# Seven half products in place of eight in the down-projection of a fused RetNet and SwiGLU kernel

## The chip, the cores and the metric

The kernel runs on one core of a Trainium2 chip. A core has TensorE (PE, matrix products, with a queue of weight loads shown as PEld), VectorE (DVE), ScalarE (ACT), GpSimd (POOL) and SyncE (SP, which issues transfers and DMA transposes). PE writes its results into PSUM, eight banks of 128 partitions by 2 KB; DVE and ACT read PSUM, POOL does not. Each engine takes its instructions strictly in the order of its own list, and waits on semaphores for the others.

The metric is the device time of one execution in microseconds (us), lower is better, as a median of several runs. The profile is of one execution, on its own clock: its span goes from the first to the last instruction.

## The reference, cut to what matters

```python
batch, n_heads, seq, head_dim = (4, 8, 768, 64)          # attention
n_tokens, d_model, d_ff = (3072, 512, 1536)              # feed-forward

def _attn_ref(q, k, v):
    gamma = 1.0 - 2.0 ** (-5.0 - np.arange(H))
    for t in range(S):
        state = gamma * state + einsum('bhd,bhe->bhde', k[:, :, t], v[:, :, t])
        y[:, :, t] = scale * einsum('bhd,bhde->bhe', q[:, :, t], state)
    return y

def _moe_ref(x, w_gate, w_val, w_out, rms_g):
    xn = x / sqrt(mean(x * x, axis=-1) + 1e-06) * rms_g
    g = xn @ w_gate
    silu = g * (1.0 / (1.0 + np.exp(-g)))
    val = xn @ w_val
    return (silu * val @ w_out)
```

`x` is the attention's output, one row of 512 values for each of the 3072 tokens. The last product, `(silu * val) @ w_out`, is the down-projection: rows of 1536 values by a 1536 x 512 matrix.

## The kernel before, in words

The sequence is cut into 6 chunks of 128 positions. Chunk c of all four batches together is **group** c: 512 tokens. For a group the attention is done in chunk form: products of queries and keys (`a`), a mask on DVE (`m0`, `m1`; tile `am`), their product with the values together with the state's share (`z`, `w`; tile `y_ps`), and the update of the state (`k`; tile `kv_ps`, with the decayed values `vp` made by `V`). Then come the mean square on ACT (`S`), its inverse root on POOL (`R`; tiles `ms`, `rstd`), the normalised rows on DVE (`N`; tile `xn`), and their transpose by DMA (`XE`; tile `xnT`).

The feed-forward part of a group is cut along d_ff into 12 slices n of 128. For each slice there is a gate product `g` and a value product `v`, each four matmuls with 512 moving columns (the tokens) and the weights as the loaded operand; `s` takes the SiLU on ACT, and `h` multiplies both on DVE into `hT`, which is [128, 12 slices, 512 tokens] in bf16.

The down-projection `d` of a batch b of the group takes, for each of the 12 slices, 128 tokens of `hT` as loaded operand and the slice's 512 columns of `wo_b` (w_out in bf16) as moving operand, and adds all 12 in one PSUM bank: 12 matmuls of 512 columns, 48 for a group. `o` copies the bank to SBUF on ACT or DVE, `st` stores it. Batch 3 of the last group is cut by columns into 192, 192 and 128 (`e`), so that the last copy and store are small.

What sets the order of the work is one text, `ORDER`, written out by hand or by a planner: a list of steps such as `d.1.2.0.12/1`, which is step `d` with c=1, b=2, slices 0 to 12, in PSUM bank 1, or `V.3.0@D`, step `V` on DVE. The program is recorded in this order, and each engine gets its share of it in this order; nothing is moved later. A step may wait for a tile that is not ready, and everything behind it on its engine waits with it.

The lines that the prediction speaks of: matmuls of `g` and `v` L665, of `d` L695, of `e` L721; `am` L471, `w` L522, `k` L485; `vp` L383, `xn` L595, `ms` and `rstd` L581 and L583; copies L142.

Of the kernel before, what the change touches and what calls it, by code (L numbers as in the profile page):

```python
# [54 lines left out]
v.2.6.7.0.4/4 g.2.7.8.0.4/5 g.2.5.6.0.4/3 g.2.4.5.0.4/6 v.2.1.2.0.4/0 R.3.0 R.3.1 h.2.6.7.0.4 N.3.1 Cq.3.2@P
h.2.1.2.0.4 N.3.0 V.3.2@P s.2.8.9.0.4 s.2.7.8.0.4 s.2.5.6.0.4 g.2.0.1.0.4/5 v.2.7.8.0.4/1 v.2.8.9.0.4/2 v.2.5.6.0.4/3
g.2.2.3.0.4/0 k.3.1/47 tq.3.3 tk.3.3 tk.3.2 Lv.4.2@S tq.3.2 Lv.5.2@S Lq.5.3@S XE.3.1@S Lq.4.0@S Cq.5.3@P V.4.2@D
h.2.5.6.0.4 h.2.7.8.0.4 u0.3.1 h.2.8.9.0.4 s.2.4.5.0.4 s.2.2.3.0.4 b0.3.1@A s.2.0.1.0.4 v.2.0.1.0.4/3 v.2.4.5.0.4/1
v.2.2.3.0.4/2 z.3.1/50 a.3.1/46 u1.3.1 h.2.4.5.0.4 m0.3.1 m1.3.1 h.2.0.1.0.4 Cq.5.2@D h.2.2.3.0.4 g.2.10.11.0.4/1
v.2.9.10.0.4/4 w.3.1 g.2.9.10.0.4/3 v.2.11.12.0.4/6 v.2.10.11.0.4/2 g.2.11.12.0.4/7 S.3.2 s.2.9.10.0.4 S.3.3  # L60
s.2.10.11.0.4 s.2.11.12.0.4 Lk.4.3@P R.3.2 R.3.3 N.3.2 h.2.9.10.0.4 N.3.3 h.2.10.11.0.4 h.2.11.12.0.4 Lv.5.3@S
XE.3.0@S tq.4.1 Lv.4.0@S st.0.0@S XE.3.2@S Lv.4.1@S XE.3.3@S st.0.1@S Lv.4.3@S Lq.4.2@S d.2.1.0.10/4 d.2.1.10.12
d.2.2.0.12/6 d.2.3.0.12/2 g.3.11.12.0.4/7 v.3.0.1.0.4/0 g.3.0.1.0.4/1 g.3.6.7.0.4/5 g.3.10.11.0.4/3 st.0.3@S Lq.4.3@S
tk.4.0 st.1.0@S o.2.3@A s.3.6.7.0.4 o.2.2@A s.3.0.1.0.4 V.5.3@D o.2.1@A V.4.3@D h.3.0.1.0.4 V.4.1@P s.3.11.12.0.4
s.3.10.11.0.4 g.3.3.4.0.4/5 g.3.2.3.0.4/6 v.3.11.12.0.4/4 v.3.10.11.0.4/3 v.3.6.7.0.4/7 g.3.4.5.0.4/0 v.3.3.4.0.4/1
g.3.1.2.0.4/2 Cq.4.3@D h.3.10.11.0.4 h.3.11.12.0.4 V.4.0@D h.3.6.7.0.4 s.3.3.4.0.4 s.3.4.5.0.4 s.3.1.2.0.4 Cq.4.2@P
# [30 lines left out]
def kernel(  # L97
# [11 lines left out]
    nc = tc.nc  # L109
# [88 lines left out]
    def ring(shape, dtype, name, bufs):  # L198
        return sb.tile(shape, dtype, name=name, bufs=bufs)
# [506 lines left out]
    def st(e, bk, c, b, i=None):  # L706
# [4 lines left out]
        else:  # L711
            e.dma_start(out=out_h[c, b // 2, b % 2][:, :, m], in_=x)


    CUT = (0, 192, 384, 512)

    @op
    def e(e, bk, c, b, i):
# [42 lines left out]
```

## Time and profile before

| | us |
|---|---|
| median of 3 runs | 228.56 (228.42 to 229.04) |
| span of the profiled execution | 227.3 |
| PE busy | 221.2 (97%) |
| DVE busy | 121.5 (53%) |
| ACT busy | 88.0 (39%) |
| POOL busy | 88.2 (39%) |
| mean granted clock of PE | 1.000 |

The profiled execution's own time is known by its span alone: 227.3 us, 1.26 us below the median of the runs shown. Busy times are sums over an engine's instructions; a matmul's listed duration (380 ns for 512 columns) holds its way through a pipeline, so the pace of matmuls is read from the chain, where a row gives the time that so many took one behind the other.

### The profile page before, as it was taken

What the parts mean: (1) busy time and instruction counts of PE and PEld (TensorE: products, weight loads), DVE (VectorE), ACT (ScalarE), POOL (GpSimd) and SP (SyncE); (2) the same over time, 40 slices, a digit from 0 to 9 for tenths busy, and PEclk for the clock granted to TensorE, in tenths of its full rate; (3) what the DMA queues carried; (4) which work ended last, traced back from release to release, by engine and by line L of the source; (5) the groups of instructions that cost most, each with busy time, mean ns of one, the idle gap of its engine ahead of it and who ended that gap; (6) DMA issues with size and microseconds to landing.
All of it is one profiled execution on the core that took longest, in us unless ns stands there. A gap on an engine that the chain in (4) does not pass through costs nothing.

```text
span 227.3 us, 5786 instructions
## 1 busy us (share of the span) xinstructions
PE 221.2 (97%) x2410; PEld 115.0 (51%) x2410; DVE 121.5 (53%) x224; ACT 88.0 (39%) x192; POOL 88.2 (39%) x137
## 2 busy tenths in 40 slices
PE   7899999999999999999999999999999999999994
PEld 2577854565455644444444445544554444444453
DVE  6495459946388685247751377850564543052211
ACT  7798323341525540724411545251452232152011
POOL 8899897746632640743225803170031000000000
PEclk9999999999999999999999999999999999999999
DMA  6999999999999986999969999556003400220116
GB/s 130 174 164 180 197 172 193 177 187 200 186 145 159 182 119 146 248 143 219 154 163 257 163 159 218 130 102 136 2 6 87 144 0 4 91 92 0 46 52 227
DMA packets 105355, 31.57 MB, mean 139 GB/s; under 512 B 94449, under 2 KB 102385, under 8 KB 105330
## 3 DMA queue, kind: packets, MB, share of 16 engines
q0 software_dynamic: 40112, 9.70, 46.4%
q1 hardware_dynamic: 65218, 21.51, 44.1%
q8 instruction: 19, 0.31, 0.6%
q14 instruction: 6, 0.05, 0.1%
HBM read 28.31 MB, written 6.29 MB: 152 GB/s over the span
## 4 chain that ended last, share of the span: by engine, by line
PE 87%; DMA 4%; DVE 2%; issue 2%; POOL 2%; SPq 0%; ACT 0%; POOLq 0%
PE g_ps L665 26%; PE v_ps L665 26%; PE o_ps L695 25%; DMA qb<-in_q_dram 2%; DMA qf<-in_q_dram 2%; PE o_ps L721 1%; DVE am L535 1%; PE kv_ps L485 1%; PE a_ps L428 1%; PE y_ps L522 1%; PE y_ps L506 1%; PE y_ps L550 1%; PE t_ps L396 1%; PE t_ps L391 1%; PE xt_ps L608 1%
## 5 line engine op out<-in xcount | busy, mean ns | idle before, releaser
L665 PE MATMUL v_ps<-xnT,wv_b 128*128 128x512 bf16 (+2 forms) x344 | 70.0, 345 | 0.0
L665 PE MATMUL g_ps<-xnT,wg_b 128*128 128x512 bf16 (+2 forms) x344 | 69.7, 345 | 0.0
L676 ACT ACTIVATE sg<-g_ps 128x512 bf16<-128x512 f32 (+2 forms) x76 | 41.9, 577 | 67.0 <-PE g_ps L665 54.4
L695 PE MATMUL o_ps<-wo_b,hT 128*128 128x512 bf16 x276 | 62.6, 380 | 0.0
L686 DVE TENSOR_TENSOR hT<-sg,v_ps 128x512 bf16<-128x512 bf16 x48 | 32.8, 723 | 38.7 <-ACT sg L676 19.4
L665 PEld LDWEIGHTS <-wv_b 128*128 128x128 bf16 x344 | 30.8, 98 | 30.2 <-DVE hT L686 0.4
L665 PEld LDWEIGHTS <-wg_b 128*128 128x128 bf16 x344 | 30.3, 98 | 29.3 <-DVE st_f L494 0.2
L695 PEld LDWEIGHTS <-hT 128*128 128x128 bf16 x276 | 26.2, 98 | 29.8
L595 DVE SCALAR_TENSOR_TENSOR xn<-y_ps,rstd,g_bc 128x512 bf16<-128x512 f32 x24 | 17.6, 746 | 12.7 <-POOL rstd L583 12.1
L688 DVE TENSOR_TENSOR hT<-sg,v_ps 128x512 bf16<-128x512 bf16 (+2 forms) x28 | 16.6, 606 | 14.6 <-PE v_ps L665 7.5
L364 POOL TENSOR_TENSOR qb<-qf,ydec 128x512 bf16<-128x512 f32 x13 | 13.7, 1065 | 26.9 <-DMA qf<-in_q_dram 26.9
L142 ACT COPY o_sb<-o_ps 128x512 f32<-128x512 f32 (+2 forms) x17 | 9.2, 553 | 36.6 <-PE o_ps L695 32.3
L567 ACT ACTIVATE xsq<-y_ps 128x512 f32<-128x512 f32 x24 | 14.2, 596 | 21.6 <-PE y_ps L506 16.2
L336 POOL DMA_DIRECT2D kb<-in_k_dram x20 | 18.2, 911 | 2.6 <-DMA wo_b<-in_moe_w_out_dram 1.4
L581 POOL TENSOR_SCALAR ms<-ssq 128x1 f32<-128x1 f32 x21 | 4.4, 212 | 35.1 <-ACT xsq L567 30.0
L471 DVE TENSOR_TENSOR am<-a_ps,causal_h 128x512 bf16<-128x512 f32 x16 | 10.6, 684 | 8.9 <-PE a_ps L462 8.9
L142 DVE COPY o_sb<-o_ps 128x512 f32<-128x512 f32 (+1 forms) x9 | 5.7, 647 | 13.8 <-PE v_ps L665 4.8
L583 POOL TENSOR_TENSOR rstd<-ms,mhalf 128x1 f32<-128x1 f32 x21 | 11.6, 551 | 1.7
L535 DVE TENSOR_TENSOR am<-a_ps,mask 128x512 bf16<-128x512 f32 x16 | 10.2, 681 | 2.4 <-PE a_ps L428 2.3
L383 POOL TENSOR_TENSOR vp<-vf,vdec 128x512 bf16<-128x512 f32 x7 | 7.3, 1050 | 7.9 <-DMA vf<-in_v_dram 7.9
L383 DVE TENSOR_TENSOR vp<-vf,vdec 128x512 bf16<-128x512 f32 x9 | 6.2, 692 | 4.5 <-DMA vf<-in_v_dram 4.5
L229 PE MATMUL hot_ps<-one 128*128 128x512 bf16 x16 | 6.2, 523 | 1.0 <-DVE one L149 1.0
(99 smaller groups left out, 166.4 us busy)
## 6 DMA issues: line engine op xcount, KB each, us to landing
out_dram<-o_sb SPq DMA_DIRECT2D x23, 256.0 KB, 2.4
vf<-in_v_dram SPq DMA_DIRECT2D x17, 256.0 KB, 3.6
qf<-in_q_dram SPq DMA_DIRECT2D x16, 256.0 KB, 4.1
kb<-in_k_dram POOLq DMA_DIRECT2D x23, 128.0 KB, 6.1
wo_b<-in_moe_w_out_dram POOLq DMA_DIRECT2D x3, 512.0 KB, 10.7
qb<-in_q_dram POOLq DMA_DIRECT2D x8, 128.0 KB, 7.4
vp<-in_v_dram POOLq DMA_DIRECT2D x7, 128.0 KB, 10.1
wv_b<-in_moe_w_val_dram POOLq DMA_DIRECT2D x3, 256.0 KB, 6.2
```

What stands on the lines that cost most here:

```text
L142: return (e.copy if e is ACT else e.tensor_copy)(out, in_)
L336: i = done[n, c, b] = e.dma_start(out=x, in_=rows[n][b, c])
L364: e.tensor_tensor(out=u["qb"], in0=u["qf"], in1=ydec[:, c, :, None].to_broadcast([128, H, D]), op=ALU.mult)
L383: e.tensor_tensor(out=u["vp"], in0=u["vf"], in1=vdec[:, c, :, None].to_broadcast([128, H, D]), op=ALU.mult)
L535: return DVE.tensor_tensor(out=u["am"][:, i], in0=u["a"][i], in1=m, op=ALU.mult)
L567: return ACT.activation(xsq, flat(u["y"]), AF.Square, accum_out=u["ssq"])
L595: return DVE.scalar_tensor_tensor(out=u["xn"], in0=flat(u["y"]), scalar=u["rstd"], in1=g_bc, op0=ALU.mult, op1=ALU.mult)
L665: r = nc.tensor.matmul(p[:, (n - n0) * m:(n - n0 + 1) * m], W[w][0][:, s, n * 128:(n + 1) * 128], xnT[c][:, s, b0 * C:b1 * C], start=s == ...
L676: return ACT.activation(sg[:, :cols], done["wg", c, n0, b0][:, :cols], AF.Silu)
L686: return DVE.tensor_tensor(out=out, in0=sg, in1=p, op=ALU.mult)
L688: return DVE.tensor_tensor(out=hT[c][:, n0:n1, b0 * C:b1 * C], in0=sg, in1=p, op=ALU.mult)
L695: nc.tensor.matmul(o_ps[c, b], hT[c][:, n, b * C:(b + 1) * C], wo_b[:, n, :], start=n == 0, stop=n == NFF - 1)
```

## The change

It replaces the down-projection of groups 2 to 5. Groups 0 and 1 keep theirs.

For a group, the 512 rows of the product are cut into two halves of 256 tokens (i), the 1536 summed elements into two halves of 6 slices (k), and the 512 output columns into two halves of 256 (j). With A_ik for the blocks of `hT` and B_kj for those of `wo_b`, the output block C_ij is A_i1 B_1j + A_i2 B_2j: eight half products in all. Strassen's scheme, in Winograd's form, needs seven:

- Four sums of weights, once: T1 = B12 - B11, T2 = B22 - T1, T3 = B22 - B12, T4 = B21 - T2 (`tw`, 6 x 256 elements on 128 partitions each, on DVE).
- Four sums of rows for each group: S1 = A21 + A22, S2 = S1 - A11, S3 = A11 - A21 (in place of A21), S4 = A12 - S2 (in place of A12) (`ss`, in two or three pieces, on DVE or POOL). All are bf16 in SBUF.
- Seven products (`p`): P1 = A11 B11, P2 = A12 B21, P3 = S4 B22, P4 = A22 T4, P5 = S1 T1, P6 = S2 T2, P7 = S3 T3. Each is 6 slices by 2 blocks of 128 tokens: 12 matmuls with 256 moving columns and a loaded block each. 84 matmuls for a group in place of 48.
- The assembly (`r`): products that belong together add up in one of three PSUM banks, and what the banks hold midway is taken out: `r.1` copies P1 (ACT), `r.6` adds P6 to it, `r.67` adds P7 as well, `r.11` copies P1 + P2 to the output block, `r.22`, `r.12` and `r.21` add a bank and a part to output blocks. The additions are on DVE: two of 512 elements and six of 256 for each group, all f32.

For the last group `p` and `r` are done for each block of 128 tokens alone (`p.1.5.0.1`, `p.1.5.1.2`), `ss` in three pieces, and the stores by halves of 256 columns. The steps `d`, `o` for groups 2 to 5 and all of `e` are gone.

The room for the sums comes from sharing: the masks, the query decay and two helper rows of groups 0 and 1 are now one tile, whose place the weight sums take later; the state of groups 0 and 1 shares its place with the row sums.

`ORDER` has the same steps in the same order up to the copies of group 1's outputs, with the four `tw` put in (PSUM banks are numbered differently throughout, one for one); behind that it is written anew.

The first place is DVE's list near 79 us of the profile. Before (`am` the masked scores, `vp` the decayed values, `xn` the normalised rows):

```order
L471 TENSOR_TENSOR am<-a_ps,causal_h 128x512
L688 TENSOR_TENSOR hT<-sg,v_ps 128x512
L383 TENSOR_TENSOR vp<-vf,vdec 128x512
L595 SCALAR_TENSOR_TENSOR xn<-y_ps,rstd,g_bc 128x512
L471 TENSOR_TENSOR am<-a_ps,causal_h 128x512
L595 SCALAR_TENSOR_TENSOR xn<-y_ps,rstd,g_bc 128x512
L383 TENSOR_TENSOR vp<-vf,vdec 128x512
```

And of the change (`wsum` holds the four weight sums):

```order
L693 TENSOR_TENSOR hT<-sg,v_ps 128x512
L390 TENSOR_TENSOR vp<-vf,vdec 128x512
L740 TENSOR_TENSOR wsum<-wo_b 128x1536
L740 TENSOR_TENSOR wsum<-wo_b,wsum 128x1536
L740 TENSOR_TENSOR wsum<-wo_b 128x1536
L740 TENSOR_TENSOR wsum<-wo_b,wsum 128x1536
L602 SCALAR_TENSOR_TENSOR xn<-y_ps,rstd,g_bc 128x512
L478 TENSOR_TENSOR am<-a_ps,causal_h 128x512
L602 SCALAR_TENSOR_TENSOR xn<-y_ps,rstd,g_bc 128x512
L390 TENSOR_TENSOR vp<-vf,vdec 128x512
```

The four sums stand between `V.3.0` and `N.2.0`; the rows around them are the same ones.

The second place is the end of group 2's feed-forward part, where its row sums are made (`ssum` holds S1 and S2, `part` what is taken out of the banks midway). DVE's list of the change:

```order
L760 TENSOR_TENSOR ssum<-hT 128x1024
L760 TENSOR_TENSOR hT<-hT 128x4x256
L693 TENSOR_TENSOR hT<-sg,v_ps 128x4x2x64 x2
L760 TENSOR_TENSOR ssum<-hT 128x512
L390 TENSOR_TENSOR vp<-vf,vdec 128x512
L760 TENSOR_TENSOR ssum<-ssum,hT 128x1024
L789 TENSOR_TENSOR part_2480<-p_ps,part_2433 128x512
```

and POOL's at the same place:

```order
L590 TENSOR_TENSOR rstd<-ms,mhalf 128x1
L760 TENSOR_TENSOR hT<-hT 128x2x256
L760 TENSOR_TENSOR ssum<-ssum,hT 128x512
L390 TENSOR_TENSOR vp<-vf,vdec 128x512
L371 TENSOR_TENSOR qb<-qf,ydec 128x512
```

Before, neither engine had sums of rows. Now the last two `hT` of the group are followed by S1's last third, a `vp`, and S2's first part on DVE, while POOL makes the last third of S3 and S2 (`ss.3.2.4.6`, `ss.2.2.4.6`).

The diff, cut to its core (of `ORDER`, the line with the `tw` and the last two lines stand for the rest):

```diff
 ORDER = """
...
+V.3.0@D tw.1@D tw.2@D tw.3@D tw.4@D N.2.0 m0.2.1 N.2.1 V.3.1@D XE.2.1@S XE.2.0@S v.1.0.4.3.4/6 g.1.0.4.3.4/4
...
+ss.4.5.0.2@P p.3.5.0.1 st.5.3.1@S p.3.5.1.2 r.12.5.0.1 p.4.5.0.1 st.5.0.1@S r.12.5.1.2 st.5.1.1@S r.21.5.0.1 st.5.2.0@S
+p.4.5.1.2 r.21.5.1.2 st.5.3.0@S
 """
...
-    mask0 = const.tile([128, 2, NHP, C], F32, name="mask0")
-    mask1 = const.tile([128, 2, NHP, C], F32, name="mask1")
-    qdec = const.tile([128, NHP, C], F32, name="qdec")
+    early = const.tile([128, shared], F32, name="early", tag="shared")
...
-    CUT = (0, 192, 384, 512)
-
-    @op
-    def e(e, bk, c, b, i):
...
+    CUT = (0, DM // 2, DM)
+    sums, prod = {}, {}
+
+    @op
+    def tw(e, bk, i):
+        if "T" not in sums:
+            sums["T"] = const.tile([128, 4, NF2, DM // 2], BF16, name="wsum", tag="shared")
+        b11, b12, b21, b22 = (wo_b[:, f, m] for f in (F0, F1) for m in (M0, M1))
+        t1, t2, t3, t4 = (sums["T"][:, j] for j in range(4))
+        out, x, y = ((t1, b12, b11), (t2, b22, t1), (t3, b22, b12), (t4, b21, t2))[i - 1]
+        return e.tensor_tensor(out=out, in0=x, in1=y, op=ALU.subtract)
...
+    @op
+    def ss(e, bk, i, c, n0, n1):
+        f1 = slice(NF2 + n0, NF2 + n1)
+        (a11, a21), (a12, a22) = ([hT[c][:, f, m] for m in (slice(0, GT // 2), slice(GT // 2, GT))] for f in (slice(n0, n1), f1))
+        s1, s2 = row_sum(1, c, n0, n1) if i < 3 else None, row_sum(2, c, n0, n1) if i != 3 and i > 1 else None
+        out, x, y, f = ((s1, a21, a22, ALU.add), (s2, s1, a11, ALU.subtract), (a21, a11, a21, ALU.subtract),
+                        (a12, a12, s2, ALU.subtract))[i - 1]
+        return e.tensor_tensor(out=out, in0=x, in1=y, op=f)
+
+    INTO = {1: 1, 2: 1, 11: 1, 6: 2, 7: 2, 4: 2, 67: 2, 21: 2, 5: 3, 3: 3, 22: 3, 12: 3}
+
+    @op
+    def p(e, bk, i, c, j0=0, j1=2, n0=0, n1=NFF // 2):
+        if bk:
+            prod[INTO[i], c, j0] = bank(bk[0], [128, j1 - j0, DM // 2], F32, "p_ps")
...
+        for n in range(n0, n1):
+            l, off, r = {1: (h0, 0, w0[:, :, M0]), 2: (h1, 0, w1[:, :, M0]), 3: (h1, 0, w1[:, :, M1]), 4: (h1, k, t[:, 3]),
+                         5: (None, 1, t[:, 0]), 6: (None, 2, t[:, 1]), 7: (h0, k, t[:, 2])}[i]
+            z = row_sum(off, c, n, n + 1)[:, 0] if l is None else l[:, n, off:off + k]
+            for j in range(j0, j1):
+                nc.tensor.matmul(x[:, j - j0], z[:, j * C:(j + 1) * C], r[:, n],
+                                 start=i in (1, 5, 6) and n == 0 and j == j0, stop=n == NF2 - 1, skip_group_check=True)
+
+    @op
+    def r(e, bk, i, c, j0=0, j1=2, j=None):
+        x = prod[INTO[i], c, j0]
...
+        if i in (1, 6, 67):
+            y = part(i)[:, j0:j1]
+            return copy(e, y, x) if i == 1 else DVE.tensor_tensor(out=y, in0=x, in1=z, op=ALU.add)
+        for n in range(j0, j1):
...
+            if i == 11:
+                copy(e, y, x[:, n - j0])
+            else:
+                DVE.tensor_tensor(out=y, in0=x[:, n - j0], in1=z[:, n - j0], op=ALU.add)
```

More of the change, by code (lines that the diff above doesn't have):

```diff
@@ L172 @@
     ydec = const.tile([128, NCH, H], F32, name="ydec")
-    mask0 = const.tile([128, 2, NHP, C], F32, name="mask0")
-    mask1 = const.tile([128, 2, NHP, C], F32, name="mask1")
-    qdec = const.tile([128, NHP, C], F32, name="qdec")
-    row_m = const.tile([128, C], F32, name="row_m")
+    shared = NFF // 2 * DM
+    early = const.tile([128, shared], F32, name="early", tag="shared")
+    mask0, mask1 = (early[:, i * H * C:(i + 1) * H * C].rearrange("p (i hp c) -> p i hp c", i=2, hp=NHP) for i in range(2))
+    qdec = early[:, 2 * H * C:2 * H * C + NHP * C].rearrange("p (hp c) -> p hp c", hp=NHP)
+    row_m, below = (early[:, 2 * H * C + (NHP + i) * C:2 * H * C + (NHP + i + 1) * C] for i in range(2))
     lngp = const.tile([128, NHP], F32, name="lngp")
@@ L187 @@
     causal_h = const.tile([128, HC], BF16, name="causal_h")
-    st_b = [const.tile([128, NHP, 2 * D], BF16, name=f"st_b{b}") for b in range(B)]
+    st_all = const.tile([128, 6, NHP, 2 * D], BF16, name="st_b", tag="shared_st")
+    st_b = [st_all[:, b] for b in range(B)]
     t = {(c, b): {} for c in range(NCH) for b in range(B)}
@@ L712, in st @@
             e.dma_start(out=out_h[c, b // 2, b % 2][:, :, m], in_=x)
-    CUT = (0, 192, 384, 512)
-    @op
-    def e(e, bk, c, b, i):
-        p = o_ps[c, b, i] = bank(bk[0], [128, CUT[i + 1] - CUT[i]], F32, "o_ps")
-        for n in range(NFF):
-            nc.tensor.matmul(p, hT[c][:, n, b * C:(b + 1) * C], wo_b[:, n, CUT[i]:CUT[i + 1]],
-                             start=n == 0, stop=n == NFF - 1)
+    NF2 = NFF // 2
+    F0, F1 = slice(0, NF2), slice(NF2, NFF)
+    M0, M1 = slice(0, DM // 2), slice(DM // 2, DM)
@@ new lines, in row_sum, with part @@
+    def row_sum(i, c, n0, n1):
+        if "S" not in sums:
+            sums["S"] = const.tile([128, 2, NF2, GT // 2], BF16, name="ssum", tag="shared_st")
+        return sums["S"][:, i - 1, n0:n1]
+    def part(i):
+        if ("s", i) not in prod:
+            pool, tag = {1: (sb, "kf"), 6: (const, "shared_g"), 67: (const, "part")}[i]
+            prod["s", i] = pool.tile([128, 2, DM // 2], F32, name=f"part{i}", bufs=1, tag=tag)
+        return prod["s", i]
+    @op
[6 more added lines that the diff above has]
+        return e.tensor_tensor(out=out, in0=x, in1=y, op=f)
@@ new lines @@
+    INTO = {1: 1, 2: 1, 11: 1, 6: 2, 7: 2, 4: 2, 67: 2, 21: 2, 5: 3, 3: 3, 22: 3, 12: 3}
[3 more added lines that the diff above has]
+            prod[INTO[i], c, j0] = bank(bk[0], [128, j1 - j0, DM // 2], F32, "p_ps")
+        x, t = prod[INTO[i], c, j0], sums["T"]
+        h0, h1 = hT[c][:, :NF2], hT[c][:, NF2:]
+        w0, w1 = wo_b[:, :NF2], wo_b[:, NF2:]
+        k = GT // 2
+        for n in range(n0, n1):
[5 more added lines that the diff above has]
+                                 start=i in (1, 5, 6) and n == 0 and j == j0, stop=n == NF2 - 1, skip_group_check=True)
@@ new lines, in r @@
+    @op
+    def r(e, bk, i, c, j0=0, j1=2, j=None):
+        x = prod[INTO[i], c, j0]
+        if j is not None:
+            x, j0, j1 = x[:, j - j0:j - j0 + 1], j, j + 1
+        z = {6: 1, 67: 1, 21: 1, 22: 67, 12: 6}.get(i)
+        z = z and part(z)[:, j0:j1]
+        if i in (1, 6, 67):
+            y = part(i)[:, j0:j1]
+            return copy(e, y, x) if i == 1 else DVE.tensor_tensor(out=y, in0=x, in1=z, op=ALU.add)
+        for n in range(j0, j1):
+            b = 2 * (i // 10 - 1) + n
+            if ("o", c, b) not in done:
+                done["o", c, b] = ring([128, DM], F32, "o_sb", 6)
+            y = done["o", c, b][:, (M0, M1)[i % 10 - 1]]
+            if i == 11:
+                copy(e, y, x[:, n - j0])
+            else:
+                DVE.tensor_tensor(out=y, in0=x[:, n - j0], in1=z[:, n - j0], op=ALU.add)
```

156 lines of the change are left out of this document (79 added, 77 removed).

## The prediction

> **What bounds the kernel now.** I read the page first, then the table of windows, then the chain, then the timelines of three engines around 80 us.
>
> ```profile
> span 227.3 us, 5786 instructions
> PE 221.2 (97%) x2410; PEld 115.0 (51%) x2410; DVE 121.5 (53%) x224; ACT 88.0 (39%) x192; POOL 88.2 (39%) x137
> PE 87%; DMA 4%; DVE 2%; issue 2%; POOL 2%; SPq 0%; ACT 0%; POOLq 0%
> ...
> 80.00:100.00 20.00, 19.64 (x258) 9.41 (x257) 10.25 (x16) 7.89 (x18) 8.96 (x14) 1.00 1.00 162
> 100.00:120.00 20.00, 20.00 (x214) 9.23 (x212) 12.93 (x20) 5.86 (x12) 4.46 (x7) 1.00 0.91 181
> 180.00:200.00 20.00, 20.00 (x95) 9.01 (x93) 5.96 (x10) 5.95 (x11) 0.00 (x0) 1.00 0.07 27
> ```
>
> TensorE is busy 97% of the span and holds 87% of the chain. In the windows (stretch, its length, then busy us of PE, PEld, DVE, ACT, POOL) it is full from 100 us on and lacks 0.36 us between 80 and 100. So behind 80 us every microsecond of TensorE work that goes shortens the kernel by as much, and every new wait of TensorE lengthens it by as much. DVE has half of its time free, which says nothing yet on where it is late.
>
> **The matmuls.** The chain prices them (start, length, what):
>
> ```profile
> 24.76 0.89 PE v_ps L665 x16
> 114.41 7.77 PE o_ps L695 x36
> 215.68 0.99 PE o_ps L721 x12
> 222.28 1.67 PE o_ps L721 x24
> ...
> L665 PEld LDWEIGHTS <-wg_b 128*128 128x128 bf16 x344 | 30.3, 98 | 29.3 <-DVE st_f L494 0.2
> ```
>
> 128 moving columns cost 0.89/16 = 0.0556 us, 192 cost 0.99/12 = 0.0825, 512 cost 7.77/36 = 0.2158. The line through the outer two gives 0.109 for 256, a width that the kernel has not run. A weight load is 98 ns long, but at 128 columns every matmul has its own load and still takes 0.0556, so the 84 loads of a group hide behind 256 columns; were they bare, the price would be gone.
> Before, groups 2 to 4 take 48 x 0.2158 = 10.36 us each and group 5 takes 36 x 0.2158 + 0.99 + 1.67 = 10.43. After, each takes 7 x 12 = 84 matmuls, 84 x 0.109 = 9.16. Saved: 3 x 1.20 + 1.27 = **4.87 us**.
>
> **The weight sums.** Four sums of 1536 elements go into DVE's queue between `V.3.0` and `N.2.0`. The timelines there (start, length, engine, line, [idle before]):
>
> ```profile
> 78.69 2.75 PE L695 MATMUL o_ps<-wo_b,hT 128*128 128x512 bf16 x12
> 81.38 0.45 PE L522 MATMUL y_ps<-vp,am 64*64 64x64 bf16 x32
> 82.34 0.41 PE L485 MATMUL kv_ps<-vp,kb 64*64 64x64 bf16 x28 [0.36 <-DVE vp L383]
> ...
> 78.23 0.68 DVE L383 TENSOR_TENSOR vp<-vf,vdec 128x512 bf16<-128x512 f32 x1
> 79.63 0.75 DVE L595 SCALAR_TENSOR_TENSOR xn<-y_ps,rstd,g_bc 128x512 bf16<-128x512 f32 x1 [0.72 <-POOL rstd L583]
> 80.30 0.68 DVE L471 TENSOR_TENSOR am<-a_ps,causal_h 128x512 bf16<-128x512 f32 x1
> 80.90 0.74 DVE L595 SCALAR_TENSOR_TENSOR xn<-y_ps,rstd,g_bc 128x512 bf16<-128x512 f32 x1
> 81.56 0.73 DVE L383 TENSOR_TENSOR vp<-vf,vdec 128x512 bf16<-128x512 f32 x1
> ...
> 78.30 0.67 POOL L581 TENSOR_SCALAR ms<-ssq 128x1 f32<-128x1 f32 x1
> 79.05 0.55 POOL L583 TENSOR_TENSOR rstd<-ms,mhalf 128x1 f32<-128x1 f32 x1
> 80.70 1.04 POOL L383 TENSOR_TENSOR vp<-vf,vdec 128x512 bf16<-128x512 f32 x1 [1.10 <-DMA vf<-in_v_dram]
> 82.86 0.19 POOL L581 TENSOR_SCALAR ms<-ssq 128x1 f32<-128x1 f32 x1 [1.11 <-ACT xsq L567]
> ```
>
> Behind the sums stand `N.2.0` (79.63), `m0.2.1` (80.30), `N.2.1` and `V.3.1` (81.56). TensorE's `w.2.1` (81.38) needs the `am` of 80.30, and its `k.3.0` needs the `vp` of 81.56: that is the 0.36 of today. The cover is thin: DVE is idle for 0.72 us, and TensorE's queue holds nothing else before `w.2.1`. So a delay of DVE reaches `k.3.0` whole, and TensorE stays full behind it: nothing gives it back.
>
> What do the sums cost? No row adds two bf16 tiles in SBUF.
>
> ```profile
> L142 DVE COPY xnT<-xt_ps 128x512 bf16<-128x512 bf16 x6 | 2.4, 417 | 0.0
> L383 DVE TENSOR_TENSOR vp<-vf,vdec 128x512 bf16<-128x512 f32 x9 | 6.2, 692 | 4.5 <-DMA vf<-in_v_dram 4.5
> L688 DVE TENSOR_TENSOR hT<-sg,v_ps 128x256 bf16<-128x256 bf16 x4 | 1.7, 419 | 4.7 <-PE t_ps L396 2.9 <-ACT sg L676 1.8
> ```
>
> Each two-input row here has an f32 operand. From 256 to 512 elements these go from 419 to about 690 ns: 1.05 ns an element and 150 ns fixed. The copy, 16 bits on both sides, does 512 in 417, half the slope. So a sum of 1536 takes 1.75 us at the one pace and 0.95 at the other. I take 0.95, since both inputs and the output are bf16, as in the copy.
> The Trainium skill (VectorE: DVE Perf Modes, section "The perf-mode tier table") has tensor_tensor on bf16 in SBUF at two elements a cycle, 1224 ns for 2048, so by estimate 0.92 us for 1536; no run here shows it yet. By that page the sum below holds; by the two-input f32 rows alone it would be 2.5 us or more worse, the slower rival.
>
> Neighbours on DVE start 0.08 us before the one ahead ends (80.30 + 0.68 against 80.90). `tw.1` starts at 78.83; three further at 0.87 and one wait on `tw.1`'s own result give 3.6 us, so `N.2.0` starts at 82.4, **2.8 us** late. At the slow pace it is 6.0.
> And POOL wants the same port:
>
> ```profile
> 36.77 1.04 POOL L630 TENSOR_TENSOR kd<-kb,vdec 128x512 bf16<-128x512 bf16 x1
> 36.87 1.48 DVE L630 TENSOR_TENSOR kd<-kb,vdec 128x512 bf16<-128x512 bf16 x1
> ```
>
> Two two-input sums from SBUF at once took turns: DVE's 0.68 became 1.48, ending 0.54 behind POOL's. (The 0.67 of `ms` at 78.30 is the 0.19 of 82.86, held behind DVE's `vp`.) In the sums fall POOL's `rstd` (0.55) and `vp` (1.04). Between 0 and 1.6 us of this lands on DVE; I take 0.7, since POOL waits too. The delay is 2.8 to 4.4, taken as **+3.5 us**.
>
> **The row sums and the assembly.** Per group, eight pieces of row sums, and eight additions from PSUM on DVE for four copies. They lie beside matmuls unless a half product wants them early. Group 2 is the tight place.
>
> ```profile
> L676 ACT ACTIVATE sg<-g_ps 128x512 bf16<-128x512 f32 x64 | 37.0, 599 | 60.4 <-PE g_ps L665 47.8 <-DVE hT L686 11.9 <-DVE qT L405 0.5
> L686 DVE TENSOR_TENSOR hT<-sg,v_ps 128x512 bf16<-128x512 bf16 x48 | 32.8, 723 | 38.7 <-ACT sg L676 19.4 <-PE v_ps L665 19.1
> ```
>
> Counted from the end of its last gate matmul: SiLU 0.60, `hT` 0.72, first sum of 512 (0.42) done at 1.9, `V.4.2` 2.5, `ss.2.2.0.4` (1024 elements, 0.69) 3.1; POOL's two sums of 512 cost 1.05 each by its `vp` row, from 1.9 on, in turns with DVE: done between 4.0 and 5.3. TensorE runs p.1, p.5, p.2 (3 x 1.31 = 3.9) and p.6 wants POOL's third at 4.8. So 0 to 0.5 by these prices, and up to 2 if all four take turns and DVE runs at one element a cycle. I take **+0.5**. In group 3, counted from the end of its last value matmul, DVE has `hT` at 1.1, `ss.1` 1.75, two `am` 2.95 and `ss.2` 3.6; TensorE has two `w` at 0.45 (row at 81.38), `z` and `a` taken alike, and p.1 and p.5 (2.6) ahead of p.6, which so starts near 4.0. Later p.4 finds `r.67.3`, behind four `xn` of 0.75, about 0.1 late: **+0.1**, 1 to 1.5 at the slow pace. In group 4 the 2.1 us of POOL's 1024-element sum lie under four FFN matmul groups (3.5 us): 0, and 2 if those were gone. The shared buffers cost 0: up to this place each engine's list has the same waits, bank names aside.
>
> **The tail.**
>
> ```profile
> 223.97 0.27 ACT o_sb L142
> 221.63 3.26 SPq L712 DMA_DIRECT2D out_dram<-o_sb  x5
> out_dram<-o_sb SPq DMA_DIRECT2D x23, 256.0 KB, 2.4
> out_dram<-o_sb SPq DMA_DIRECT2D x1, 64.0 KB, 1.9
> ```
>
> Today a 0.27 us copy and a 64 KB store (1.9 us) follow the last matmul. Then it is a 256-column addition (0.42) and 128 KB, between 1.9 and 2.4. The stores are issued 3.26/5 = 0.65 us apart, as fast as a product of one block (6 x 0.109) yields them; one queued store adds 0.65. Between +0.2 and +0.9; **+0.35**.
>
> **Sum.** -4.87 + 3.5 + 0.5 + 0.1 + 0.35 = -0.42 us: span 226.9. The median of 228.56 is 1.26 above the profiled span; that part I leave alone. **228.1 us.** With all low ends (2.8, 0, 0, 0.2) the span falls by 1.9, 226.7 us; with all high ends of the fast pace (4.4, 2, 0.1, 0.9) it grows by 2.5, 231.1 us.
>
> **Rivals.**
> *The hole is small* (faster): POOL loses every turn, and group 2's sums arrive in time: -4.87 + 2.8 + 0.1 + 0.2 = -1.8, 226.8 us. For it: POOL's 0.67 at 78.30, where POOL waited. Against: 36.87, where DVE did. 0.20.
> *The sums run at one element a cycle* (slower): the sum above turns zero where the hole is 3.9, so from 1.0 us for a weight sum on (4 x 1.0 + 0.7 of POOL - 0.8 up to 79.63) the hole decides. -4.87 + 6.8 + 1.5 + 1.2 + 0.4 = +5.0, 233.6 us. For it: every two-input row. Against: none of them is all bf16. 0.10.
> *The clock falls in the hole* (slower):
>
> ```profile
> 1.04 4.02 PE L229 MATMUL hot_ps<-one 128*128 128x512 bf16 x9 [1.04 <-DVE one L149]
> ```
>
> The first nine 512-column matmuls, after idleness, take 4.02 us, 0.45 each for 0.2158. If a hole of 2.4 to 4 us brings that back for another 4 us, 2 us are lost: 230.1 us. Against: no later idle stretch is long enough to tell. 0.10.
> The Trainium skill (TensorE: Matmul & The Clock Gate, "Part 1") states a halved clock after an idle window of about 3.4 us; by that rule the hole must be over 3.4 us, its upper third. The granted clock stands at 1.00 in every window here, so the trace is silent on it.
> *POOL's share of the row sums is late* (slower): from the point at which POOL's sums of 512 end over 1.5 us behind p.6 in groups 2 and 3, two holes of 1 to 1.5 replace the 0.6 of the sum: 230 us. For it: POOL's 1.05 where DVE needs 0.42. 0.12.
>
> **How the numbers follow.** Forecast 0.48, its own range 227.3 to 229.0; rivals 0.20, 0.10, 0.10, 0.12. About 0.3% is what a measurement of this kernel can tell from no change: below 227.87 or above 229.25. Of the forecast's 0.48, 0.20 lie below the first, 0.27 between, 0.01 above. Faster 0.20 + 0.20 = 0.40; slower 0.01 + 0.10 + 0.10 + 0.09 = 0.30; same 0.30. The range runs from 226.5 (hole small) to 231.0 (clock, POOL), and leaves out the slow pace and little else.
>
> **What would show it.** The `p_ps` matmuls at 0.109 us and PE busy near 216.3 us; the `wsum` rows at 0.95 each; at 81.4 us a PE hole of some 3 us put down to DVE; a wait on POOL before `ssum` weights in group 2; DVE last, not ACT. A time under 226.5 would mean that the hole is not there; over 231, that a sum costs twice what I took.

## The result, and the profile after

The changed kernel takes 232.31 us (median of four, 231.57 to 232.96) against 228.68 us of the kernel before: 1.0153 times, interval 1.0130 to 1.0177. It is slower. The forecast of 228.1 us and its range (226.5 to 231.0) both missed. A single run more than 1.5% above the fastest of its kernel counts in the medians of times, but not in ratios, spans and clocks.

The profiled run of the changed kernel took 231.91 us, of which the span is 229.2. From its page, the span, the busy time of the engines, and two rows of the forty slices (5.73 us each), TensorE's busy tenths and its granted clock:

```profile
span 229.2 us, 6077 instructions
PE 217.4 (95%) x2504; PEld 128.0 (56%) x2530; DVE 154.1 (67%) x283; ACT 85.6 (37%) x188; POOL 108.3 (47%) x151
PE   7999999999999939999999999999899999999993
PEclk9999999999999997999999999999999999999999
```

TensorE has 3.8 us less to do than before (221.2), and the span is 1.9 us longer (227.3 before). Slice 15 (80.2 to 86.0 us) is only three tenths full, and behind it stands the one clock digit that is not a 9. There the timelines of TensorE, VectorE and GpSimd read (start, length, engine, line, [idle before]):

```profile
78.24 2.75 PE L702 MATMUL o_ps<-wo_b,hT 128*128 128x512 bf16 x11
84.25 0.45 PE L529 MATMUL y_ps<-vp,am 64*64 64x64 bf16 x32 [3.25 <-DVE am L478]
85.50 0.59 PE L492 MATMUL kv_ps<-vp,kb 64*64 64x64 bf16 x28 [0.38 <-DVE vp L390]
86.42 5.45 PE L702 MATMUL o_ps<-wo_b,hT 128*128 128x512 bf16 x19 [0.34 <-issue]
...
78.38 0.95 DVE L740 TENSOR_TENSOR wsum<-wo_b 128x1536 bf16<-128x1536 bf16 x1
79.37 0.96 DVE L740 TENSOR_TENSOR wsum<-wo_b,wsum 128x1536 bf16<-128x1536 bf16 x1
80.24 1.82 DVE L740 TENSOR_TENSOR wsum<-wo_b 128x1536 bf16<-128x1536 bf16 x1
81.99 0.94 DVE L740 TENSOR_TENSOR wsum<-wo_b,wsum 128x1536 bf16<-128x1536 bf16 x1
82.86 0.74 DVE L602 SCALAR_TENSOR_TENSOR xn<-y_ps,rstd,g_bc 128x512 bf16<-128x512 f32 x1
83.52 0.67 DVE L478 TENSOR_TENSOR am<-a_ps,causal_h 128x512 bf16<-128x512 f32 x1
...
80.21 1.04 POOL L390 TENSOR_TENSOR vp<-vf,vdec 128x512 bf16<-128x512 f32 x1 [0.47 <-DMA vf<-in_v_dram]
```

The four weight sums stand in front of the `am` of 83.52, and TensorE waits 3.25 us for it. The third sum started beside GpSimd's `vp` and took 1.82 us for 0.95. The matmuls behind the wait are slow as well: d.1.1 and d.1.0 are 20 matmuls, of which the trace has 19 (the first one's record is missing, hence the 0.34 us of idle time in that row). At 0.2158 us each the 19 would take 4.10 us, and they hold TensorE from 86.42 to 91.80, 5.38 us. The windows of one microsecond show why (stretch, length, PE busy, granted clock, DMA share, GB/s):

```profile
84.00:85.00 1.00, 0.67 (x52) 1.00 0.00 0
85.00:86.00 1.00, 0.62 (x32) 0.70 0.00 0
86.00:87.00 1.00, 0.67 (x9) 0.50 0.58 131
87.00:88.00 1.00, 1.00 (x4) 0.50 0.57 131
88.00:89.00 1.00, 1.00 (x4) 0.59 0.34 76
89.00:90.00 1.00, 1.00 (x7) 1.00 0.26 56
```

The granted clock is 0.50 from about 85.4 to 88.8 us: it falls 4.4 us after the wait began and 1.15 us after it ended. TensorE is back at work by then, and so the wait is paid a second time. Over the whole span the mean clock of the four runs is 0.992, 0.990, 0.985 and 0.982. Taken as a loss, (1 - clock) x span, that is 1.8, 2.3, 3.5 and 4.2 us, 2.9 in the mean. For the run with a trace, the first, the one stretch from 85.4 to 88.8 us accounts for it: 3.4 us at half the clock lose 1.7.

The half products themselves run as priced. TensorE in group 2 (the last of the four waits), and then where group 4 begins:

```profile
118.81 1.47 PE L777 MATMUL p_ps<-wo_b,hT 128*128 128x256 bf16 x12
120.12 1.47 PE L777 MATMUL p_ps<-wsum,ssum 128*128 128x256 bf16 x12
121.43 1.47 PE L777 MATMUL p_ps<-wo_b,hT 128*128 128x256 bf16 x12
123.14 1.62 PE L777 MATMUL p_ps<-wsum,ssum 128*128 128x256 bf16 x12 [0.24 <-DVE ssum L760]
...
164.40 3.61 PE L672 MATMUL g_ps<-xnT,wg_b 128*128 128x512 bf16 x15 [0.66 <-DMA xnT<-xn]
```

From start to start twelve matmuls take 1.31 us, 0.109 each. Product 6 should have begun at 122.74 and ended its 1.31 us at 124.05; it ended at 124.60, 0.55 late. And the first gate matmul of group 4 waits 0.66 us for its transposes, a wait that the kernel before did not have.

### The profile page after: what moved, and what is told of

It is laid out like the page before. It is cut to its first block, busy times and chain, and to the rows that moved or that the text cites. A ratio compares the mean times of both kernels' runs of the same rounds, so it can differ in the third digit from the quotient of the medians.

```text
span 229.2 us, 6077 instructions
## 1 busy us (share of the span) xinstructions
PE 217.4 (95%) x2504; PEld 128.0 (56%) x2530; DVE 154.1 (67%) x283; ACT 85.6 (37%) x188; POOL 108.3 (47%) x151
## 4 chain that ended last, share of the span: by engine, by line
PE 74%; DMA 9%; DVE 8%; issue 4%; POOL 3%; SPq 1%; ACT 0%; POOLq 0%; DVEq 0%; ACTq 0%
PE g_ps L672 25%; PE v_ps L672 24%; PE p_ps L777 12%; PE o_ps L702 7%; DMA wg_b<-in_moe_w_gate_dram 2%; DMA qb<-in_q_dram 2%; DMA qf<-in_q_dram 2%; DMA xnT<-xn 2%; DVE xn L602 2%; DMA kb<-in_k_dram 2%; POOL rstd L590 1%; DVE wsum L740 1%; DVE hT L693 1%; PE kv_ps L492 1%; DVE ssum L760 1%
## 5 line engine op out<-in xcount | busy, mean ns | idle before, releaser
L672 PE MATMUL v_ps<-xnT,wv_b 128*128 128x512 bf16 (+2 forms) x335 | 69.0, 343 | 0.7 <-issue 0.5
L693 DVE TENSOR_TENSOR hT<-sg,v_ps 128x512 bf16<-128x512 bf16 x48 | 33.6, 726 | 26.5 <-PE v_ps L672 18.2
L777 PEld LDWEIGHTS <-hT 128*128 128x128 bf16 x240 | 23.3, 98 | 5.1 <-DVE hT L693 0.2
L702 PE MATMUL o_ps<-wo_b,hT 128*128 128x512 bf16 x91 | 22.8, 395 | 0.7 <-issue 0.5
L777 PE MATMUL p_ps<-wo_b,hT 128*128 128x256 bf16 x144 | 17.7, 273 | 0.0
L702 PEld LDWEIGHTS <-hT 128*128 128x128 bf16 x96 | 9.3, 102 | 10.4 <-issue 1.8
L760 POOL TENSOR_TENSOR hT<-hT 128x512 bf16<-128x512 bf16 x3 | 3.9, 1285 | 21.6 <-PE g_ps L672 12.8
L590 POOL TENSOR_TENSOR rstd<-ms,mhalf 128x1 f32<-128x1 f32 x21 | 12.2, 583 | 1.7
L777 PE MATMUL p_ps<-wsum,ssum 128*128 128x256 bf16 x96 | 11.8, 273 | 0.2 <-DVE ssum L760 0.2
L777 PE MATMUL p_ps<-wsum,hT 128*128 128x256 bf16 x96 | 11.8, 273 | 0.0
L760 POOL TENSOR_TENSOR ssum<-ssum,hT 128x512 bf16<-128x512 bf16 (+1 forms) x5 | 7.2, 1438 | 9.6 <-DVE ssum L760 9.4
```

Source lines behind the costliest of these rows:

```text
L590: return POOL.tensor_tensor(out=u["rstd"], in0=ms, in1=mhalf, op=ALU.pow)
L672: r = nc.tensor.matmul(p[:, (n - n0) * m:(n - n0 + 1) * m], W[w][0][:, s, n * 128:(n + 1) * 128], xnT[c][:, s, b0 * C:b1 * C], start=s == ...
L693: return DVE.tensor_tensor(out=out, in0=sg, in1=p, op=ALU.mult)
L702: nc.tensor.matmul(o_ps[c, b], hT[c][:, n, b * C:(b + 1) * C], wo_b[:, n, :], start=n == 0, stop=n == NFF - 1)
L760: return e.tensor_tensor(out=out, in0=x, in1=y, op=f)
L777: nc.tensor.matmul(x[:, j - j0], z[:, j * C:(j + 1) * C], r[:, n], start=i in (1, 5, 6) and n == 0 and j == j0, stop=n == NF2 - 1, skip_gr ...
```

## The experiments

All ratios are against runs of the kernel before on the same chip, made beside them. A span is the median over the runs compared. The kernel before had 227.0 us (227.0 to 227.1 in three sets of runs), the changed one 230.1 (229.2 to 230.9).

**1. The sums moved, all else as changed.**

```diff
-V.3.0@D tw.1@D tw.2@D tw.3@D tw.4@D N.2.0 m0.2.1 N.2.1 ...
+V.3.0@D N.2.0 m0.2.1 N.2.1 ...
-... u1.3.0 g.2.4.5.0.4/5 ...
+... u1.3.0 tw.1@D tw.2@D g.2.4.5.0.4/5 ...
-... o.1.3@D o.1.1@D v.2.4.5.0.4/1
+... o.1.3@D o.1.1@D tw.3@D tw.4@D v.2.4.5.0.4/1
```

> The changed kernel with the four weight sums moved on VectorE: two behind the second state update of group 3 (in front of a stretch that was idle for 2.43 us), two behind the last output copy of group 1 (in front of 4.18 us idle); nothing else differs. Theory (the weight sums made TensorE wait 3.6 us near 82 us, and the granted clock fell because of that wait): the wait is gone, the granted clock is 1.000, the span is 229.2 - 3.6 - 1.4 = 224.2 us (224.0 to 225.0), the time 225.4 to 226.8 us. Rival 1 (the clock falls for another reason, the stall costs its 3.6 us only): span 225.6 or more with a clock of 0.98 to 0.99, time 227.5 to 229.5. Rival 2 (the half products and the new order cost the time, not the sums' place): 230 us or more.

Measured: 227.14 us, 0.9929 (0.9894 to 0.9965) of the kernel before; span 225.35. TensorE around the old place and at the start of group 4:

```profile
81.72 0.41 PE L492 MATMUL kv_ps<-vp,kb 64*64 64x64 bf16 x28 [0.31 <-DVE vp L390]
160.42 3.61 PE L672 MATMUL g_ps<-xnT,wg_b 128*128 128x512 bf16 x16 [1.23 <-DMA xnT<-xn]
```

And the window, with the granted clock behind TensorE's busy time:

```profile
78.00:90.00 12.00, 11.51 (x178) 1.00 1.07 135
```

In this trace the wait and the fall of the clock are gone, and with them 4.75 us of span: the same half products that were 1.5% slower are 0.7% faster. Over the ten runs the mean clock is 0.995 to 1.000 in nine and 0.984 in one, whose slow stretch was not traced. The span is 0.35 above the expected band. The second row gives a reason: the wait for group 4's transposes has grown from 0.66 to 1.23 us, so what TensorE reaches earlier it partly spends there. Rival 2 falls. The time lies between the theory's band and that of rival 1, and what speaks against rival 1 is the clock.

**2. The sums alone, without half products.** The list of the kernel before, with `tw.1@D tw.2@D tw.3@D tw.4@D` put between `V.3.0@D` and `N.2.0`, and the shared tiles of the change, which make room for them; the sums are made and not used.

> The list of the kernel before, with eight half products' worth of down-projection in every group as it was, and the four weight sums put in at the place where the change has them; what they make is not used. Theory (the sums' place costs a wait of 3.6 us and the clock with it): TensorE waits some 3.3 us at the same matmuls, the clock falls to 0.98 to 0.992, time 228.7 + 3.6 + 1.4 to 4 = 233.5 to 236.5 us. Rival (the loss lies in the half products, the sums are hidden): 228.4 to 229.5 us, clock 1.000.

Measured: 234.48 us, 1.0248 (1.0183 to 1.0313); span 232.6, clock 0.985 to 0.993. TensorE's wait, and a window behind it:

```profile
83.86 0.45 PE L523 MATMUL y_ps<-vp,am 64*64 64x64 bf16 x32 [3.23 <-DVE am L472]
```

```profile
85.00:86.00 1.00, 0.88 (x29) 0.50 0.33 76
```

The same wait and the same clock of 0.50, in a kernel that has no half product: 5.6 us for four instructions at that place. Experiment 1 takes them from there and gains 4.75 us, experiment 2 puts them there and loses 5.6.

**3. The wait kept, TensorE kept busy in it.**

```diff
-d.1.2.0.12/7 w.2.1 k.3.0/15 ...
+H.15/7 d.1.2.0.12/7 w.2.1 k.3.0/15 ...
```

`H.15` is 15 matmuls of ones by ones, 512 columns each.

> The changed kernel with 15 more matmuls of 128x512 columns (ones times ones, their result is not used) ahead of the twelve of the down-projection for the third row block of group 1: at 0.216 us each they keep TensorE busy for the 3.24 us that it waited. The weight sums stay in place, so the work behind the wait comes no earlier. Theory (the clock falls because TensorE stands idle there): granted clock 1.000, the 1.4 us that the slow clock cost in the profiled run come back, span 227.8 us (227.3 to 228.3), time 228.9 to 230.2 and with less spread than the 231.6 to 233.0 of the changed kernel. Rival (the clock falls for another reason, the load or the half products): clock 0.98 to 0.992 and time 231.5 to 233 as before the edit.

Measured: 229.02 us, 0.9996 (0.9967 to 1.0026); span 227.2; the clock of the runs compared is 0.998 to 1.000. The profiled run, of 232.26 us, is a longer one, whose clock fell at another place (0.83 in the first 20 us; experiment 4 comes back to it). At the place of the sums it was 1.00:

```profile
81.61 3.40 PE L236 MATMUL hot_ps<-one 128*128 128x512 bf16 x15
85.06 2.75 PE L702 MATMUL o_ps<-wo_b,hT 128*128 128x512 bf16 x12
87.75 0.45 PE L529 MATMUL y_ps<-vp,am 64*64 64x64 bf16 x32
```

```profile
78.00:90.00 12.00, 11.57 (x244) 1.00 0.11 24
```

3.4 us of useless work in the place of 3.25 us of waiting makes the kernel 2.9 us of span shorter (230.1 to 227.2), as much as the mean clocks had said (2.9). So the fall of the clock follows from TensorE standing idle, not from what VectorE does or from the half products. Not all of the 2.9 need be the clock's: in this trace the first gate matmul of group 4 waits 0.13 us where the changed kernel's waited 0.66, so the clock's share is about 2.4 to 2.9 us, somewhat less than the idle time itself. The 1.4 us that the expectation read from the profiled run was too little, since that run had the highest clock of the four.

**4. Shorter waits: two or three sums left in place.** As experiment 1, but `tw.1@D tw.2@D`, and in a second kernel `tw.1@D tw.2@D tw.3@D`, stay behind `V.3.0@D`, and the others go behind `o.1.1@D`.

> Weight sums 1 and 2 stay where the change has them, 3 and 4 go behind the last output copy of group 1. In the changed kernel 3 and 4 took 1.82 + 0.94 us of the 3.6, so the wait of TensorE near 82 us should be about 0.9 us. Theory (a short wait does not bring the granted clock down, the one of 3.3 us did): clock 0.998 to 1.000, span 229.2 - 2.7 - 1.4 = 225.1 us (224.7 to 225.8), time 226.3 to 227.6. Rival (the clock falls by any wait at this place, in proportion): clock near 0.996, span 226.1, time 227.5 to 228.5.

> Weight sums 1 to 3 stay where the change has them, the fourth goes behind the last output copy of group 1. The wait of TensorE near 82 us should lie between the 0.9 us worked out for two sums and the 3.6 us of four: 3.6 - 0.94 = 2.7 us. With two sums the granted clock held, with four it fell to 0.86 in the stretch 78 to 90 us. Theory A (the clock falls only after about the three us of idle that four sums make): clock 0.998 to 1.000, span 225.6 + 1.8 = 227.4 us or, where the later wait for the transposes of group 4 gives part back, 226.3; time 228.1 to 229.3. Theory B (any wait over a microsecond or two brings it down): clock 0.985 to 0.993, span 228.7 to 230, time 230.5 to 232.

Measured: with two sums 227.96 us, 0.9953 (0.9931 to 0.9976), span 225.6, clock 0.998 to 1.000. With three 230.79 us, 1.0055 (1.0018 to 1.0092), span 228.35, clock 0.984 to 0.995 in seven of the eight runs compared, 1.000 in one. The time with two sums is 0.4 above the theory's band and inside the rival's, but its span and its clock are the theory's; with three the time is inside theory B's band, the span 0.35 below it. First the wait and then a window with two sums; below, the waits and the windows with three:

```profile
81.50 0.44 PE L529 MATMUL y_ps<-vp,am 64*64 64x64 bf16 x32 [0.68 <-DVE am L478]
```

```profile
83.00:84.00 1.00, 1.00 (x28) 1.00 0.57 131
```

```profile
82.27 0.45 PE L529 MATMUL y_ps<-vp,am 64*64 64x64 bf16 x32 [1.51 <-DVE am L478]
83.53 0.59 PE L492 MATMUL kv_ps<-vp,kb 64*64 64x64 bf16 x28 [0.38 <-DVE vp L390]
```

```profile
83.00:84.00 1.00, 0.62 (x32) 0.76 0.06 7
84.00:85.00 1.00, 1.00 (x14) 0.50 0.58 131
```

Theory A of the second expectation falls: the clock does not need three microseconds of idleness. A wait of 1.51 us, with small matmuls and another 0.38 us behind it, halves it as a wait of 3.25 does; 0.68 us does not. The third sum thus cost 2.75 us of span (225.6 to 228.35), of which only 0.83 is more waiting (1.51 against 0.68). But in experiment 1 a wait of 1.23 us at group 4's first gate matmul, which has 512-column matmuls behind it, left the clock at 1.00 in the profiled run.

The kept traces say what decides. Experiment 3's own trace has a fall too, near its start, behind this wait:

```profile
6.53 0.44 PE L398 MATMUL t_ps<-pick,qb 128*64 128x64 bf16 x16 [1.62 <-DMA qb<-in_q_dram]
```

In each of the twelve traces the instants at which the granted clock changes lie a whole number of stretches of 3.413 us apart; in the changed kernel they are 85.40, 88.81 and, behind TensorE's last matmul, 228.76 us. So the clock changes only at the ends of such stretches. These are the stretches at whose end it fell (stretch, length, TensorE's busy us, clock in the stretch itself, DMA share, GB/s), in the changed kernel and in experiments 2, 4 (three sums) and 3:

```profile
81.99:85.40 3.41, 0.80 (x52) 1.00 0.02 5
81.51:84.93 3.42, 0.80 (x52) 1.00 0.02 3
80.10:83.52 3.42, 1.46 (x56) 1.00 1.18 129
4.18:7.60 3.42, 1.71 (x25) 1.00 1.43 178
```

And these are the emptiest at whose end it stayed at 1.00: the end of experiment 1, the start of the second kernel of experiment 6, and group 4's wait in experiment 1:

```profile
219.98:223.39 3.41, 1.77 (x17) 1.00 0.55 190
3.79:7.20 3.41, 2.04 (x25) 1.00 1.46 188
158.54:161.95 3.41, 2.18 (x58) 1.00 0.41 80
```

The line runs at about half of a stretch: the clock fell where TensorE was busy for 1.71 us of 3.41 or less, and for 1.77 or more it did not. No stretch behind a trace's first recorded change of the clock breaks this. So the place of a wait against these stretches counts, and short waits that fall into one stretch add up; the wait of two sums leaves 2.73 and 2.96 us of work in the two stretches that it touches. The slow stretch itself was one of 3.41 us in the changed kernel and in experiments 2 and 4, but two, from 7.60 to 14.42 us, in experiment 3's trace, although TensorE was busy in both (3.36 and 3.41 us). There the loss is about 3.4 us, as much as that run's span is above the others (230.5 to 227.2). That fits the two runs of the changed kernel that lost 3.5 and 4.2 us, which have no trace, and the place of the stretches, which differs from trace to trace, fits the one run of eight with three sums whose clock stayed at 1.000. Neither is shown.

**5. The next wait: group 4's transposes.** With the sums moved, TensorE ends the second `w` of group 4 at 151.08 us, and the four transposes leave one behind the other (SyncE's queue, start and length of all four):

```profile
152.12 5.13 SPq L621 DMA_TRANSPOSE xnT<-xn  x4
```

The gate matmul began at 160.42, 3.2 us after the last had left. Instead of hurrying them, the edit begins with what needs the first two only: `gh` makes one half (two row blocks) of a gate tile's columns, in the same PSUM bank.

```diff
-... g.4.0.1.0.4/3 g.4.1.2.0.4/1 tq.5.0 tq.5.1 r.21.3 b0.5.0@A g.4.6.7.0.4/2
+... gh.4.0.0/3 gh.4.1.0/1 tq.5.0 tq.5.1 r.21.3 b0.5.0@A gh.4.6.0/2 gh.4.0.2 gh.4.1.2 gh.4.6.2
```

> The kernel with the moved weight sums, and in it the first three gate tiles of group 4 made in two halves of their columns: the halves for the first two row blocks of all three, then the other halves (24 matmuls of 256 columns in place of 12 of 512). Its first gate matmul waited 1.23 us for the four transposes of group 4, which leave 1.28 us apart. Theory (the wait is for the last two transposes, and 12 matmuls of 0.109 us = 1.3 us that need only the first two fill it): the wait falls to 0.2 us or less, span 225.3 - 1.1 = 224.2 us, time 225.8 to 226.4 against 227.1. Rival (the four transposes land together, or the halves cost more than they hide): no gain, 226.8 to 227.4.

Measured: 225.61 us, 0.9864 (0.9808 to 0.9920). Experiment 7 ran it once more: 226.18, 0.9880 (0.9845 to 0.9916). The span over both is 223.9. TensorE where group 4 begins, and the window around it:

```profile
158.31 0.30 PE L513 MATMUL y_ps<-st_h,qT 64*64 64x64 bf16 x16
158.54 3.01 PE L685 MATMUL g_ps<-xnT,wg_b 128*128 128x256 bf16 x24
161.38 1.03 PE L672 MATMUL g_ps<-xnT,wg_b 128*128 128x512 bf16 x4
```

```profile
140.00:170.00 30.00, 30.00 (x569) 1.00 0.51 118
```

No idle time is left between 140 and 170 us, and the span is 1.45 us shorter than with the moved sums. So the wait was for the last transposes alone, and the rival falls. The time is a little below the expected band. The 24 halves take 2.84 us from start to start, 0.25 more than 12 whole ones at 0.2158, but they begin at once.

**6. The row sums of group 2, alone and with the rest.**

```diff
-... ss.3.2.4.6@P V.4.2@D st.1.0@S p.1.2/0 ss.2.2.4.6@P p.5.2/4 r.1.2@A p.2.2 ss.2.2.0.4@D st.1.3@S ...
+... ss.2.2.4.6@P st.1.0@S p.1.2/0 ss.3.2.4.6@P p.5.2/4 r.1.2@A p.2.2 ss.2.2.0.4@D V.4.2@D st.1.3@S ...
```

> The kernel with the moved weight sums, and in group 2 the copy of v for the next group on VectorE placed behind the row sum that product 6 waits for, and on GpSimd that product's last sixth ahead of product 7's. Product 6 began 0.23 us late and had about 0.15 us of waits inside. Theory (VectorE's order there is what product 6 waits for): span 0.3 to 0.4 us less, 224.9, time 226.5 to 227.0 against 227.1, at the edge of what can be told. Rival (GpSimd's part comes last and is not earlier): no change in that wait.

Measured: 227.16 us, 0.9923 (0.9893 to 0.9952), against 227.14 of experiment 1. The wait before product 6 is gone, so the rival does not hold, but no time is gained that can be told, so the theory does not either. The trace has two waits that experiment 1 lacked:

```profile
100.67 1.02 PE L672 MATMUL v_ps<-xnT,wv_b 128*128 128x512 bf16 x4 [0.20 <-DVE hT L693]
131.11 1.49 PE L777 MATMUL p_ps<-wo_b,hT 128*128 128x256 bf16 x12 [0.24 <-DVE hT L760]
```

The second is product 3 of the same group, which now waits for its own row sum; the first is for an `hT` of VectorE that had itself waited for ScalarE's SiLU.

With the halves of experiment 5 too, and `V.3.1@D` put ahead of `N.2.1`:

> Moved weight sums, the halves of group 4's first gate tiles, the row sums' order of group 2, and near 81 us the copy of v that the state product of group 3 waited 0.31 us for put ahead of a normalization. Theory: the three gains add, 1.1 + 0.35 + 0.3: span 225.3 - 1.75 = 223.5 us, time 225.0 to 225.8 us, 1.4 per cent below the kernel before. Rival (the waits only move on to the next late thing): 226.3 to 227.1.

Measured: 226.17 us, 0.9870 (0.9822 to 0.9917); span 224.2, no better than the halves alone (223.9). The time lies between the theory's band (to 225.8) and the rival's (from 226.3). The three gains do not add; the trace has new waits of 0.31 and 0.23 us in place of those removed.

**7. Three more moves.** `tw.3@D` between `o.1.3@D` and `o.1.1@D`, `tw.4@D` behind `h.2.2.3.0.4`, `ss.4.2.0.4@D` from behind `r.21.2` to behind `r.22.2`, all on top of the last kernel; beside it the kernel of the halves again.

> All four earlier edits, and three more moves on VectorE into stretches that were idle in the trace: the third weight sum ahead of group 1's last output copy (2.23 us idle, and before GpSimd's two q copies, beside which it took 1.64 us), the fourth behind the last product of group 2's third tile (1.47 us idle), and the last row sum of group 2 ahead of an output sum (0.8 to 1.8 us idle). Theory (TensorE's last four waits of group 2 and 3, 0.31 + 0.24 + 0.31 + 0.23 = 1.1 us, each come from one late operation of VectorE, and these moves remove them): 224.5 to 225.1 us against 225.6 of the halves. Rival (they only move to the next late operation, as the edits before did): no difference to the halves that can be told, within 0.4 us.

> The kernel of the halves once more, unchanged, to stand beside the next one on the same chip: 225.1 to 226.2 us, 1.2 to 1.5 per cent below the kernel before.

Measured: 225.52 us, 0.9842 (0.9814 to 0.9869), span 223.65; the halves 226.18, at the end of their band. That is the fastest of all these kernels by its median, but it misses the theory's band, and 0.25 us of span below the halves (223.9) is within the rival's 0.4. The trace still has small waits:

```profile
82.83 0.45 PE L492 MATMUL kv_ps<-vp,kb 64*64 64x64 bf16 x32 [0.36 <-DVE xn L602]
114.22 1.02 PE L672 MATMUL g_ps<-xnT,wg_b 128*128 128x512 bf16 x4 [0.28 <-DVE hT L702]
```

## Why the prediction was wrong, point by point

- **The matmuls, -4.87 us: right in the price, about 1.1 us too high in the whole.** 256 columns cost 0.109 us (1.31 for twelve) and the loads hide. But TensorE's busy time is 217.4 us for the forecast 216.3. The slow clock does not explain this: the profile of experiment 1 has 217.4 as well, at a clock of 1.00 and with all 2530 matmuls on record (the changed kernel's trace lacks 26). Where the 1.1 us arise was not located.
- **The weight sums, +3.5 us: right.** 0.95, 0.96, 1.82 and 0.94 us each; the third ran beside GpSimd's `vp` of 1.04 us and took 0.87 more (for the 0.7 taken). TensorE was 0.45 us ahead of the kernel before at 78.24; relative to that its `k.3.0` came 85.50 - 82.34 + 0.45 = 3.6 us later. The Trainium skill (VectorE: DVE Perf Modes, section "The perf-mode tier table") had two elements a cycle for bf16 in SBUF, by estimate 0.92 us; the trace agrees with 0.95.
- **The clock: the step that failed.** The prediction named this rival and gave it 0.10, because no idle stretch of the old trace told how long one must be; its forecast of +3.5 us for the hole let TensorE come out of the hole at full speed. In its place the clock was at 0.50 for 3.4 us behind the hole, and the mean clock was below 1 in each of the four runs (0.982 to 0.992). The rival's price of 2.0 us fits one slow stretch (1.7 us); the mean over the runs is 2.4 to 2.9. The Trainium skill (TensorE: Matmul & The Clock Gate, "Part 1") has the clock halved after an idle window of about 3.4 us. The trace agrees with the half (0.50) and with the length (85.4 to 88.8 us is slow), but not with a window that is idle throughout: waits of 3.25 us were enough, and of 1.51 us in experiment 4. The prediction called the old trace silent because its windows show a clock of 1.00 throughout. They show 1.00 for the first nine matmuls as well, which took 4.02 us where 1.94 is the later pace; so the column says nothing ahead of the first recorded change, at 6.0 us.
- **Group 2's row sums, +0.5 us: right in size** (0.55) **and too simple in kind.** Removing the wait gained nothing that can be told (experiment 6).
- **Group 3, +0.1 us: the wait was elsewhere.** I had counted when products 6 and 4 find their sums, and they found them. But the row sums, additions and normalizations of group 3 share VectorE, and the work between group 4's second `w` and its first gate matmul, which hides the transposes, got shorter (8.1 us for 11.1); the gate matmul waited 0.66 us. The sum has no term for it.
- **The tail, +0.35 us: too high.** TensorE's last matmul ends 3.45 us before the span's end, against 3.35: +0.1.
- **The time outside the span, 1.26 us "left alone":** that was one run. In 25 runs of the kernel before it is 1.73 to 1.88 us, in the changed kernel 1.8 to 2.7. The medians compare spans of 227.0 and 230.1 us.

The terms with what they measured, the waits from the one trace and the clock over the runs: -4.87 + 3.6 + 2.9 + 0.55 + 0.66 + 0.1 = +2.9 us, against 230.1 - 227.0 = +3.1 in median spans. That this agrees so well is partly luck, since the first term is about 1.1 us too high and the clock's may be 0.5 too high. Without the wait near 82 us, the clock and group 4's wait the sum is -4.2; experiments 5 and 7, which have none of the three, reach -3.1 and -3.35. The difference is about the 1.1 us by which TensorE's busy time exceeds the forecast.

## What to carry to other kernels

A fixed cost that is paid once is best judged by where it stands: the four sums cost 5 us ahead of an operation that TensorE waits for, and next to nothing nine to thirteen microseconds later, in idle stretches that the same timeline shows. Price a wait of TensorE twice, the idle time and the slow clock behind it, as soon as it and its neighbours can leave TensorE idle for half of a stretch of 3.4 us; in these runs that cost 1.7 us or about twice as much. And when work that hides a transfer is made shorter, look at every transfer that it hid, not only at the new operations.

## What the runs showed of the hardware that was not expected

- The granted clock goes from 1.00 to 0.50 some 2.7 to 4.4 us after a wait began and 1.1 to 1.3 us after it ended (four traces), and stays there for 3.4 us (85.4 to 88.8 us in the changed kernel) or 6.8 (experiment 3's trace, 7.6 to 14.4). Its changes lie on a grid of 3.413 us, and it fell behind each stretch in which TensorE was busy for half or less (1.71 us or less; 1.77 and more did not). A wait of 1.51 us was enough.
- That costs 1.8 to 4.2 us by the mean clocks of four runs of one kernel, and makes its times spread. One slow stretch is 1.7 us, two are 3.4; whether the runs that lost 3.5 and 4.2 had two was not seen, since only one of the four has a trace.
- Useless matmuls in the place of a wait kept the clock up (experiment 3: 232.3 to 229.0 us, with the wait's own time still lost).
- One weight sum on VectorE took 1.82 us for 0.95 when GpSimd's `vp` of 1.04 us ran beside it.
